# Decode of two layers over a key-value cache: the norm's factor applied to the projections' results, and a shorter wait ahead of them

## The chip, the cores and the metric

The kernel runs on one core of a Trainium2 chip. The metric is the device time of one execution in microseconds (us). The kernel before was run nine times; its time is the median of these.

## The reference

Eight rows (B = 8, one token each, D = 448) pass two times through an attention layer and an MLP layer with the same weights. All inputs are bfloat16. Cut to what matters:

```python
def ln(x): return (x - mean(x)) / sqrt(var(x) + 1e-5)

def A(x):                       # 16 query heads, 8 key/value heads of 256, 4096 positions
    q = (x @ wq)                # 448 -> 4096
    p = softmax(q . k_cache / 16)
    return (p . v_cache) @ wo   # 4096 -> 448

def Bmlp(x):
    h  = gelu(ln(x) @ w1); hs = shifted_along_the_sequence(h) @ w2
    x1 = x + hs                 # every shift leaves a sequence of length 1
    return x1 + gelu(ln(x1) @ w3) @ w4      # 448 -> 1792 -> 448

for layer in range(2):
    x = x + A(ln(x))
    x = x + Bmlp(ln(x))
```

The sequence has length one and each of the four groups is shifted by one or two places and filled with zeros, so hs is zero and x1 = x; w1 and w2 are not read. The MLP step is therefore x + ln(x) + gelu(ln(ln(x)) @ w3) @ w4. The norm of a norm is the same centred x with another factor.

## The kernel before

**The stream.** The work is a list of 128 pairs (layer, row, key/value head). A pair needs a key and a value cache of 2 MB each, loaded in halves of 1 MB into a ring of five buffers. All loads are issued by SyncE in one order; each waits until the buffer it overwrites has been used. Of each row, nine of the sixteen key halves stay in SBUF, transposed (`keep`), from layer 0 to layer 1, so that layer 1's pairs of heads 0 to 3 load only values, and head 4 half of its keys. The list alternates such light pairs with whole ones.

**A pair** (`attend`). In eight turns TensorE transposes four blocks of keys into PSUM (`tk`, L607), and VectorE (L614) and ScalarE (L612) copy them out by turns, to `ktr` or `keep`. Then come the scores (`ps`, L631), the maximum (VectorE L678, GpSimd L681), the exponential on ScalarE (L687), the sum on GpSimd (L692), and the product with the values (`pvb`, L705), copied to `ob` (L711), turned by TensorE (L723), summed to `os` (L726) and scaled to `oT` (L730). `output` multiplies one head's `oT` by wo (L457) and VectorE adds the result to x (L463); for the first five rows of layer 1 `outputs` does this for all heads at once (L473, L480).

**The jobs.** Everything that follows a row's last pair is a generator: `mix` (the MLP) and `queries` (the next layer's q). `pump`, called after every turn, every two scores and every product with values, advances the first job by one `yield`. At each `yield` the job's instructions issued so far stand on the engines' queues ahead of the pair's next ones, and every engine runs its queue in order. `Sched.op` adds the semaphores' waits. The first queries, of all eight rows, run through (`drain`) after the first pair's keys have been transposed; the last MLP, of rows 5 to 7, runs through at the end with nothing beside it. The MLP of rows 0 to 4 in layer 1 is one job among the last row's pairs.

**The norm before** (`layernorm`, `rsqrt`, `scaled`, `lift`). VectorE squares x (L346) and sums x and its square per partition (L347); GpSimd sums over the partitions (`partition_all_reduce`, L351). VectorE forms mean and variance (L355, L357, L359), for the MLP the second factor's argument (L365), the centred x (`xc`, L369), and the reciprocal root by a bit trick and three Newton steps (L327 to L338). Then L376 writes `lnT`, the centred x times the factor, for the MLP also `t1`, the first norm's result, and L491 adds that to x (`xres`). After WAIT empty steps `project` multiplies (L417). D = 448 is held as one block of 64 rows and three of 128; the 64-row block stands in the lower half of the partitions, and half of the weights' tiles have it in the upper half. `lift` moves lnT's 64 rows up by a matmul with the identity (L404) and a copy (L407). The queries are copied from PSUM to `qT` (L436 for one row, L445 for eight); the MLP's projection to `hb` (L501), on which the GELU works (L504 to L512). L521 is the second projection and L526 its sum with `xres`. At the very end x is transposed (L780), copied (L783) and stored (L785).

Of the kernel before, what the change touches and what calls it, by code (L numbers as in the profile page):

```python
# [3 lines left out]
P = 128  # L4
B = 8
D = 448
HQ = 16
# [6 lines left out]
KC = 4  # L14
NF = F // P
LN_EPS = 1e-5
# [9 lines left out]
N_REP = 24  # L26
N_MLP = 24
RATE = 1.0
WAIT = 5
N_PS = 2  # L30
N_SPARE = 2
N_ONCE = 5
# [99 lines left out]
def decode_two_layers(nc, A_x, A_k_cache, A_v_cache, A_wq, A_wo, B_w3, B_w4, out):  # L132
# [10 lines left out]
    def sb(name, shape, dt):  # L143
        return nc.alloc_sbuf_tensor(name, shape, dt), Res()
# [25 lines left out]
    lnT, r_ln = sb("lnT", [P, KC + 1, B], bf)  # L170
    r_lift = Res()
    sm, r_sm = sb("sm", [P, 8, 2 * B], f32)
    smi, r_smi = sb("smi", [P, 2 * B], i32)
    hb, r_hb = sb("hb", [P, NF, B], f32)
    hw, r_hw = sb("hw", [P, NF, B], f32)
# [20 lines left out]
    C_Y = 0  # L196
    C_H = 32
    C_Q = 160
    C_L = 480
    C_P = 448  # L200


# [120 lines left out]

    def rsqrt(src, dst, n):

        v, y, w, hv = sm[:, src, 0:n], sm[:, dst, 0:n], sm[:, 7, 0:n], sm[:, 6, 0:n]
        op("dve", lambda e: e.tensor_single_scalar(smi[:, 0:n], v.bitcast(i32), 1, ALU.arith_shift_right),  # L327
           reads=[r_sm], writes=[r_smi])
        op("dve", lambda e: e.tensor_scalar(smi[:, 0:n], smi[:, 0:n], -1, RSQRT_MAGIC, ALU.mult, ALU.add),
           reads=[r_smi], writes=[r_smi])  # L330
        op("dve", lambda e: e.tensor_single_scalar(hv, v, -0.5, ALU.mult), reads=[r_sm], writes=[r_sm])
        yield
        y0 = smi[:, 0:n].bitcast(f32)
        for i in range(3):
            a, r_a = (y0, r_smi) if i == 0 else (y, r_sm)
            op("dve", lambda e, a=a: e.tensor_tensor(w, a, a, ALU.mult), reads=[r_a], writes=[r_sm])
            op("dve", lambda e: e.tensor_tensor(w, w, hv, ALU.mult), reads=[r_sm], writes=[r_sm])  # L337
            op("dve", lambda e, a=a: e.scalar_tensor_tensor(y, w, 1.5, a, ALU.add, ALU.mult),  # L338
               reads=[r_sm, r_a], writes=[r_sm])
            yield  # L340

    def layernorm(lo, n, twice):

        x_ = xT[:, :, lo:lo + n]
        s = lambda k, a=0: sm[:, k, a * n:(a + 1) * n]
        op("dve", lambda e: e.tensor_tensor(xx[:, 1, :, lo:lo + n], x_, x_, ALU.mult), reads=[r_x], writes=[r_x])  # L346
        op("dve", lambda e: e.tensor_reduce(sm[:, 0, 0:2 * n].rearrange("p (k n) -> p k n", k=2),  # L347
                                            xx[:, :, :, lo:lo + n].rearrange("p k c n -> p k n c"),
                                            axis=AX.X, op=ALU.add),
           reads=[r_x], writes=[r_sm])  # L350
        op("pool", lambda e: e.partition_all_reduce(sm[:, 1, 0:2 * n], sm[:, 0, 0:2 * n], P, ReduceOp.add),  # L351
           reads=[r_sm], writes=[r_sm])
        yield
        yield
        one = lambda o, *a: op("dve", lambda e: e.tensor_single_scalar(o, *a), reads=[r_sm], writes=[r_sm])  # L355
        one(sm[:, 1, 0:2 * n], sm[:, 1, 0:2 * n], 1.0 / D, ALU.mult)
        op("dve", lambda e: e.scalar_tensor_tensor(s(2), s(1), -1.0, s(1), ALU.mult, ALU.mult),  # L357
           reads=[r_sm], writes=[r_sm])
        op("dve", lambda e: e.tensor_tensor(s(2), s(2), s(1, 1), ALU.add), reads=[r_sm], writes=[r_sm])  # L359
        one(s(4), s(2), 0.0, ALU.max)  # L360
        one(s(2), s(4), LN_EPS, ALU.add)
        yield
        if twice:

            op("dve", lambda e: e.scalar_tensor_tensor(s(2, 1), s(2), LN_EPS, s(4), ALU.mult, ALU.add),  # L365
               reads=[r_sm], writes=[r_sm])

        for hi, c0, c1 in ((P, 1, 4), (64, 0, 1)):
            op("dve", lambda e, hi=hi, c0=c0, c1=c1: e.tensor_tensor(  # L369
                xc[0:hi, c0:c1, 0:n], x_[0:hi, c0:c1, :],  # L370
                s(1)[0:hi].unsqueeze(1).to_broadcast([hi, c1 - c0, n]), ALU.subtract),
               reads=[r_x, r_sm], writes=[r_xc])
        yield from rsqrt(2, 3, 2 * n if twice else n)

    def scaled(dst, r_dst, a, n):
        op("dve", lambda e: e.tensor_tensor(dst[:, 0:KC, 0:n], xc[:, :, 0:n],  # L376
                                            bc(sm[:, 3, a * n:(a + 1) * n], n), ALU.mult),
           reads=[r_xc, r_sm], writes=[r_dst])

    def kr(kc):  # L380
        return P if kc > 0 else 64
# [17 lines left out]
            return w3[:, kc - 1, t * P:(t + 1) * P]  # L399
        return w3f[:, t % (NF // 2) * P:(t % (NF // 2) + 1) * P]  # L400

    def lift(n):

        op("pe", lambda e: e.matmul(mm[64:P, C_L:C_L + n], ident[0:64, 0:64], lnT[0:64, 0, 0:n],  # L404
                                    start=True, stop=True, skip_group_check=True),
           reads=[r_ident, r_ln], writes=[r_mm])
        op("dve", lambda e: e.tensor_copy(lnT[64:P, KC, 0:n], mm[64:P, C_L:C_L + n]),  # L407
           reads=[r_mm], writes=[r_lift])

    def project(cols, r_w, at, ts, upper, n):  # L410

        def f(e):
# [9 lines left out]
    def queries(lo, n):  # L422

        yield from layernorm(lo, n, False)
        scaled(lnT, r_ln, 0, n)
        for _ in range(WAIT):
            yield
        for h in range(HKV):
            for t in (4 * h, 4 * h + 2):
                project(wq_cols, wq_r, C_Q, range(t, t + 2), t >= 16, n)  # L430
                if t == 0:
                    lift(n)
                yield
            if n > 1:
                continue
            op("dve", lambda e, h=h: e.tensor_copy(  # L436
                qT[:, lo, :, 2 * h:2 * h + 2],
                mm[:, C_Q + 4 * h * B:C_Q + 4 * (h + 1) * B].rearrange("p (a c n) -> p n c a", n=B, c=2)[:, 0, :, :]),
               reads=[r_mm], writes=[r_q[lo][h]])
            ready[lo] = h + 1  # L440
            yield
            yield
        for c in range(2):
            if n > 1:
                op("dve", lambda e, c=c: e.tensor_copy(  # L445
                    qT[:, lo:lo + n, c, :],
                    mm[:, C_Q:C_Q + 32 * B].rearrange("p (a c n) -> p n c a", n=B, c=2)[:, 0:n, c, :]),
                   reads=[r_mm], writes=[r for b in range(lo, lo + n) for r in r_q[b]])

    def output(b, h):  # L450

# [31 lines left out]
    def mix(lo, n):  # L483

        y_ = mm[:, C_Y:C_Y + KC * B].rearrange("p (c n) -> p c n", n=B)[:, :, lo:lo + n]
        x_ = xT[:, :, lo:lo + n]
        yield from layernorm(lo, n, True)
        scaled(lnT, r_ln, 1, n)

        scaled(t1, r_t1, 0, n)  # L490
        op("dve", lambda e: e.tensor_tensor(xres[:, :, 0:n], x_, t1[:, :, 0:n], ALU.add),  # L491
           reads=[r_x, r_t1], writes=[r_xres])
        for _ in range(WAIT):
            yield
        for ts in (range(0, 2), range(2, 4), range(4, 7), range(7, 9), range(9, 11), range(11, 14)):
            project(w3_cols, w3_r, C_H, ts, ts[0] >= NF // 2, n)
            if ts[0] == 0:
                lift(n)
            yield
        h_, w_ = hb[:, :, 0:n], hw[:, :, 0:n]  # L500
        op("dve", lambda e: e.tensor_copy(  # L501
            h_, mm[:, C_H:C_H + NF * B].rearrange("p (t n) -> p t n", n=B)[:, :, 0:n]),
           reads=[r_mm], writes=[r_hb])
        op("dve", lambda e: e.scalar_tensor_tensor(w_, h_, GELU_C, h_, ALU.mult, ALU.mult),  # L504
           reads=[r_hb], writes=[r_hw])
        op("dve", lambda e: e.scalar_tensor_tensor(w_, w_, 1.0, h_, ALU.add, ALU.mult),
           reads=[r_hb, r_hw], writes=[r_hw])
        op("act", lambda e: e.activation(w_, w_, ACT.Tanh, scale=GELU_K), reads=[r_hw], writes=[r_hw])
        yield
        yield  # L510

        op("dve", lambda e: e.scalar_tensor_tensor(hT[:, :, 0:n], w_, 1.0, h_, ALU.add, ALU.mult),  # L512
           reads=[r_hb, r_hw], writes=[r_hT])
        yield
        yield
        for c in range(KC):
            def f(e, c=c):
                w = kr(c)
                last = None
                for t in range(NF):  # L520
                    last = e.matmul(room(w, C_Y + c * B + lo, n), w4[:, t, row0(c):row0(c) + w],  # L521
                                    copies(hT[:, t, 0:n], n), start=(t == 0), stop=(t == NF - 1), skip_group_check=True)
                return last
            op("pe", f, reads=[r_w4, r_hT], writes=[r_mm])
            yield
        op("dve", lambda e: e.scalar_tensor_tensor(x_, y_, 0.5, xres[:, :, 0:n], ALU.mult, ALU.add),  # L526
           reads=[r_mm, r_xres], writes=[r_x])
        yield
# [313 lines left out]
```

## Time and profile before

| | |
|---|---|
| median of nine runs | 1179.08 us (1178.33 to 1181.07) |
| the profiled execution | 1181.07 us, its span 1179.3 us |
| mean granted TensorE clock | 0.944 |
| TensorE busy (matmuls) | 947.2 us, 80% |
| VectorE busy | 490.7 us, 42%, 1819 instructions |
| ScalarE busy | 312.4 us, 26% |
| GpSimd busy | 105.4 us, 9% |
| transfers | 474.70 MB, mean 403 GB/s over the span |
| chain that ended last | DMA 47%, TensorE 36%, VectorE 10% |

The span runs from the first to the last instruction of the execution that the hardware profiler took. Busy times of engines overlap. In the profile PE is TensorE's matmuls, PEld its weight loads, DVE VectorE, ACT ScalarE, POOL GpSimd, SP SyncE; L417 is line 417 of the kernel before. In the changed kernel the same code has other line numbers.

### The profile page before, as it was taken

How to read it: one execution, taken by the hardware profiler on the slowest of the kernel's cores; microseconds unless marked ns; L12 is line 12 of the kernel's file. 1: busy time of each engine (PE TensorE's matmuls, PEld its weight loads, DVE VectorE, ACT ScalarE, POOL GpSimd, SP SyncE). 2: the span in 40 equal slices, each digit the busy share in tenths (PEclk: the TensorE clock that was granted, in tenths of full speed). 3: DMA queues.
4: the chain of work that ended last, by engine and by line, in shares of the span. 5: the costliest groups of instructions: out<-in, count | busy, mean ns of one | idle time of the engine just before them, and what ended most of it. 6: DMA issues, size and time to landing. Idle time of an engine off the chain costs nothing.

```text
span 1179.3 us, 42729 instructions
## 1 busy us (share of the span) xinstructions
PE 947.2 (80%) x19323; PEld 823.7 (70%) x19323; DVE 490.7 (42%) x1819; ACT 312.4 (26%) x891; POOL 105.4 (9%) x281
## 2 busy tenths in 40 slices
PE   2777888778877888778877887878877898888895
PEld 2766777667766776667766776767766777777784
DVE  2324543345333543354333533354334533454343
ACT  1223322223223222222222222232222222322220
POOL 0000001101001011001100011001110011001100
PEclk8879989899989999999999899999899998999896
DMA  9999999999999999999999999999999999999893
GB/s 351 384 416 420 419 387 420 419 420 419 417 417 416 412 420 405 419 420 411 417 416 420 384 395 413 419 420 413 413 419 420 404 409 419 419 418 395 350 402 144
DMA packets 70678, 474.70 MB, mean 403 GB/s; under 512 B 7248, under 2 KB 13280, under 8 KB 13792
## 3 DMA queue, kind: packets, MB, share of 16 engines
q1 hardware_dynamic: 70496, 471.97, 97.9%
q8 instruction: 151, 2.47, 0.8%
q14 instruction: 31, 0.25, 0.1%
HBM read 471.93 MB, written 0.01 MB: 400 GB/s over the span
## 4 chain that ended last, share of the span: by engine, by line
DMA 47%; PE 36%; DVE 10%; issue 5%; POOL 1%; ACT 0%; SPq 0%; POOLq 0%; ACTq 0%
DMA ring<-in_A_k_cache_dram 47%; PE tk L607 16%; PE ps L631 7%; PE pvb L705 5%; PE mm L457 3%; DVE ktr L614 3%; PE mm L417 2%; PE mm L521 1%; PE pvb L723 1%; DVE keep L614 1%; DVE oT L730 1%; DVE sm L355 1%; DVE os L726 1%; DVE sm L337 1%; DVE sm L338 1%
## 5 line engine op out<-in xcount | busy, mean ns | idle before, releaser
L607 PE MATMUL tk<-ident,ring 128*128 128x128 f32 x2944 | 412.5, 293 | 126.7 <-DMA ring<-in_A_k_cache_dram 125.2
L607 PEld LDWEIGHTS tk<-ident,ring 128*128 128x128 f32 x2944 | 347.2, 150 | 170.6 <-DMA ring<-in_A_k_cache_dram 161.6
L614 DVE COPY ktr<-tk 128x512 f32<-128x512 f32 x224 | 153.9, 690 | 187.9 <-PE tk L607 187.3
L612 ACT COPY ktr<-tk 128x512 f32<-128x512 f32 x224 | 129.9, 586 | 326.4 <-PE tk L607 326.3
L705 PE MATMUL pvb<-ring,pT 128*2 128x256 bf16 x4096 | 161.2, 277 | 31.0 <-DMA ring<-in_A_v_cache_dram 18.7
L631 PE MATMUL ps<-qT,keep 128*128 128x48 bf16 x4608 | 160.9, 184 | 5.7 <-issue 4.7
L631 PEld LDWEIGHTS ps<-qT,keep 128*128 128x128 bf16 x4608 | 145.7, 97 | 17.1 <-issue 11.2
L614 DVE COPY keep<-tk 128x512 f32<-128x512 f32 x144 | 99.6, 691 | 138.7 <-PE tk L607 138.0
L612 ACT COPY keep<-tk 128x512 f32<-128x512 f32 x144 | 84.4, 586 | 244.5 <-PE tk L607 244.5
L687 ACT ACTIVATE pT<-ps,nb 128x32 bf16<-128x32 f32 x256 | 76.6, 299 | 272.6 <-DVE nb L683 226.3
L631 PE MATMUL ps<-qT,ktr 128*128 128x48 bf16 x3584 | 129.9, 184 | 15.1 <-DVE ktr L614 6.7
L631 PEld LDWEIGHTS ps<-qT,ktr 128*128 128x128 bf16 x3584 | 115.5, 97 | 26.3 <-DVE ktr L614 18.5
L681 POOL PARTITION_ALL_REDUCE gm<-pm x128 | 45.6, 357 | 793.2 <-DVE pm L678 793.2
L705 PEld LDWEIGHTS pvb<-ring,pT 128*2 128x2 bf16 x4096 | 76.3, 82 | 55.5 <-DMA ring<-in_A_v_cache_dram 23.6
L457 PE MATMUL mm<-oT,wo_sb 128*128 128x24 bf16 (+1 forms) x1408 | 64.2, 187 | 11.9 <-DVE oT L730 6.0
L711 DVE COPY ob<-pvb 128x256 f32<-128x256 f32 x128 | 53.8, 420 | 42.0 <-PE pvb L705 41.3
L457 PEld LDWEIGHTS mm<-oT,wo_sb 128*128 128x128 bf16 (+1 forms) x1408 | 51.5, 101 | 24.6 <-DVE oT L730 20.7
L692 POOL PARTITION_ALL_REDUCE dn<-rs x128 | 51.3, 400 | 151.0 <-ACT pT L687 151.0
L723 PE MATMUL pvb<-ident,ob 128*128 128x128 f32 x256 | 53.7, 293 | 6.8 <-DVE ob L711 6.6
L678 DVE TENSOR_REDUCE pm<-ps 128x2 f32<-128x64 f32 x128 | 28.7, 224 | 70.0 <-PE ps L631 69.4
L417 PE MATMUL mm<-lnT,wq_sb 128*128 128x24 bf16 x864 | 48.5, 184 | 11.6 <-DVE lnT L376 9.1
L417 PEld LDWEIGHTS mm<-lnT,wq_sb 128*128 128x128 bf16 x864 | 40.3, 99 | 20.9 <-DVE lnT L376 9.4
(70 smaller groups left out, 491.0 us busy)
## 6 DMA issues: line engine op xcount, KB each, us to landing
ring<-in_A_v_cache_dram SPq DMA_DIRECT2D x256, 1024.0 KB, 10.3
ring<-in_A_k_cache_dram SPq DMA_DIRECT2D x184, 1024.0 KB, 10.5
wo_sb<-in_A_wo_dram SPq DMA_DIRECT2D x1, 3584.0 KB, 25.6
wq_sb<-in_A_wq_dram SPq DMA_DIRECT2D x3, 1024.0 KB, 11.5
w_sb<-in_B_w_dram SPq DMA_DIRECT2D x1, 1568.0 KB, 20.4
w_sb<-in_B_w_dram SPq DMA_DIRECT2D x3, 448.0 KB, 13.2
wqf_sb<-in_A_wq_dram SPq DMA_DIRECT2D x2, 256.0 KB, 14.9
w3f_sb<-in_B_w_dram SPq DMA_DIRECT2D x2, 112.0 KB, 14.3
```

The costliest lines, as they stand in the source:

```text
L417: last = e.matmul(room(P, at + t * B, n), cols(kc, t), copies(rhs, n), start=(kc == 1), stop=(kc == 0), skip_group_check=True)
L457: last = e.matmul(room(w, C_P + c, 1), wo[:, t, row0(c):row0(c) + w], copies(oT[:, t // 2, t % 2, b:b + 1], 1), start=(t == 4 * h), stop=( ...
L607: last = e.transpose(bank[:, j * P:(j + 1) * P], src[:, 4 * (f % 4) + j, :].bitcast(f32), ident4[:, :])
L612: op("act", lambda e: e.copy(flat, bank[:, :]), reads=[r_bank], writes=[r_kt])
L614: op("dve", lambda e: e.tensor_copy(flat, bank[:, :]), reads=[r_bank], writes=[r_kt])
L631: last = e.matmul(pst[:, at:at + 2 * N_REP].rearrange("p (r j) -> p r j", j=2), kt(i, c), repeated(qT[:, b, c, 2 * h:2 * h + 2]), start=(c ...
L681: op("pool", lambda e: e.partition_all_reduce(gm[q][0][:, :], pm[q][0][:, :], P, ReduceOp.max), reads=[pm[q][1]], writes=[gm[q][1]])
L687: return e.activation(pT[q][0][:, :, :].rearrange("p i j -> p j i")[:, j, :], pst[:, C_S:C_S + 2 * NI].rearrange("p (i j) -> p j i", j=2)[ ...
L692: op("pool", lambda e: e.partition_all_reduce(dn[q][0][:, :], rs[q][0][:, :], P, ReduceOp.add), reads=[rs[q][1]], writes=[dn[q][1]])
L705: last = e.matmul(pvb[at:at + 2, 0:DH], pT[q][0][:, a * HALF + i, :], v[:, i, :], start=(a == 0 and i < 4), stop=(a == 1 and i >= HALF - 4 ...
L711: op("dve", lambda e: e.tensor_copy(ob[:, :], pvb[:, 0:DH]), reads=[r_pv], writes=[r_ob])
L723: last = e.transpose(pvb[:, DH + c * P:DH + (c + 1) * P], ob[:, c * P:(c + 1) * P], ident4[:, :])
```

## The change

The order of the pairs, the ring, the loads and the split of the last MLP into five rows and three are the same in both kernels. What differs is the norm and what uses it.

- GpSimd's sum goes to a tile of its own, `sg`. `centered` forms x minus the mean from it and writes it straight into `lnT`, without the factor, ahead of the variance and the root. The projections run on that.
- The factor, one for each row, is multiplied into the projections' results: the copies to `qT` and `hb` become multiplications by it.
- `lift` goes. VectorE writes the upper 64 partitions of the lifted block itself, in two instructions of 32 partitions each.
- Five instructions of the variance become three, and the Newton step multiplies by -0.5 in passing, so that one instruction ahead of it goes.
- In `mix` the first norm's result and its sum with x are formed behind `hT`, from a second call of `centered`.
- WAIT, the empty steps ahead of the projections, goes from 5 to 3; `layernorm` with `rsqrt` has one more step than before.

```diff
-WAIT = 5
+WAIT = 3
...
+    sg, r_sg = sb("sg", [P, 2 * B], f32)
...
     def rsqrt(src, dst, n):
...
-        op("dve", lambda e: e.tensor_single_scalar(hv, v, -0.5, ALU.mult), reads=[r_sm], writes=[r_sm])
...
-            op("dve", lambda e: e.tensor_tensor(w, w, hv, ALU.mult), reads=[r_sm], writes=[r_sm])
+            op("dve", lambda e: e.scalar_tensor_tensor(w, w, -0.5, v, ALU.mult, ALU.mult), reads=[r_sm], writes=[r_sm])
...
     def layernorm(lo, n, twice):
...
-        op("pool", lambda e: e.partition_all_reduce(sm[:, 1, 0:2 * n], sm[:, 0, 0:2 * n], P, ReduceOp.add),
-           reads=[r_sm], writes=[r_sm])
-        yield
-        yield
-        (five instructions: mean, variance, clamp, eps)
-        yield
+        op("pool", lambda e: e.partition_all_reduce(sg[:, 0:2 * n], sm[:, 0, 0:2 * n], P, ReduceOp.add),
+           reads=[r_sm], writes=[r_sg])
+        yield
+        yield
+        centered(lnT, r_ln, lo, n)
+        yield
+        (three instructions: variance, clamp and eps)
+        for p in (0, 32):
+            op("dve", lambda e, p=p: e.scalar_tensor_tensor(
+                lnT[64 + p:96 + p, KC, 0:n], sg[p:p + 32, 0:n], -1.0 / D, x_[p:p + 32, 0, :], ALU.mult, ALU.add),
+               reads=[r_x, r_sg], writes=[r_lift])
         if twice:
+            op("dve", lambda e: e.tensor_single_scalar(s(4), s(4), 0.0, ALU.max), reads=[r_sm], writes=[r_sm])
             op("dve", lambda e: e.scalar_tensor_tensor(s(2, 1), s(2), LN_EPS, s(4), ALU.mult, ALU.add),
                reads=[r_sm], writes=[r_sm])
-        (two instructions that centre x into xc)
+        yield
         yield from rsqrt(2, 3, 2 * n if twice else n)
+
+    def centered(dst, r_dst, lo, n):
+        for hi, c0, c1 in ((P, 1, 4), (64, 0, 1)):
+            op("dve", lambda e, hi=hi, c0=c0, c1=c1: e.scalar_tensor_tensor(
+                dst[0:hi, c0:c1, 0:n], sg[0:hi, 0:n].unsqueeze(1).to_broadcast([hi, c1 - c0, n]), -1.0 / D,
+                xT[0:hi, c0:c1, lo:lo + n], ALU.mult, ALU.add),
+               reads=[r_x, r_sg], writes=[r_dst])
...
-    def scaled(dst, r_dst, a, n):
-    def lift(n):
...
     def queries(lo, n):
         yield from layernorm(lo, n, False)
-        scaled(lnT, r_ln, 0, n)
         for _ in range(WAIT):
             yield
...
-                if t == 0:
-                    lift(n)
...
-            op("dve", lambda e, h=h: e.tensor_copy(
+            op("dve", lambda e, h=h: e.tensor_tensor(
                 qT[:, lo, :, 2 * h:2 * h + 2],
                 mm[:, C_Q + 4 * h * B:...],
+                sm[:, 3, 0:1].unsqueeze(2).to_broadcast([P, 2, 2]), ALU.mult),
...
     def mix(lo, n):
         yield from layernorm(lo, n, True)
-        scaled(lnT, r_ln, 1, n)
-        scaled(t1, r_t1, 0, n)
-        op("dve", lambda e: e.tensor_tensor(xres[:, :, 0:n], x_, t1[:, :, 0:n], ALU.add),
-           reads=[r_x, r_t1], writes=[r_xres])
         for _ in range(WAIT):
             yield
...
-            if ts[0] == 0:
-                lift(n)
...
-        op("dve", lambda e: e.tensor_copy(h_, mm[:, C_H:...]), reads=[r_mm], writes=[r_hb])
+        op("dve", lambda e: e.tensor_tensor(h_, mm[:, C_H:...],
+            sm[:, 3, n:2 * n].unsqueeze(1).to_broadcast([P, NF, n]), ALU.mult),
+           reads=[r_mm, r_sm], writes=[r_hb])
...
         op("dve", lambda e: e.scalar_tensor_tensor(hT[:, :, 0:n], w_, 1.0, h_, ALU.add, ALU.mult),
            reads=[r_hb, r_hw], writes=[r_hT])
         yield
+        centered(xc, r_xc, lo, n)
+        op("dve", lambda e: e.tensor_tensor(t1[:, :, 0:n], xc[:, :, 0:n], bc(sm[:, 3, 0:n], n), ALU.mult),
+           reads=[r_xc, r_sm], writes=[r_t1])
+        op("dve", lambda e: e.tensor_tensor(xres[:, :, 0:n], x_, t1[:, :, 0:n], ALU.add),
+           reads=[r_x, r_t1], writes=[r_xres])
         yield
```

## The prediction

> **What bounds the kernel now.** I read the page's slices first, to see where the transfers run, then a table of windows for the stretches where they do not, then the chain of waits through the end, then the timelines of the start and of the one large hole, and last the list of waits.
>
> The page's slices of DMA share and of throughput:
>
> ```profile
> DMA  9999999999999999999999999999999999999893
> GB/s 351 384 416 420 419 387 420 419 420 419 417 417 416 412 420 405 419 420 411 417 416 420 384 395 413 419 420 413 413 419 420 404 409 419 419 418 395 350 402 144
> ```
>
> Each slice is 29.5 us. The DMA engines are full in all slices but two: the kernel is a stream of 472 MB that runs at about 420 GB/s when nothing holds it back, and what can be won is the stretch without transfers at the end, the hole in the 38th slice, and a few per cent where the rate drops.
>
> The table of windows (us, then busy time of PE, PEld, DVE, ACT and POOL, then granted clock, DMA share, GB/s):
>
> ```profile
> 30.00:45.00 15.00, 13.97 (x254) 12.80 (x252) 6.13 (x16) 4.85 (x14) 1.54 (x4) 0.80 1.06 393
> 150.00:195.00 45.00, 40.32 (x835) 35.92 (x832) 19.69 (x80) 11.79 (x34) 4.18 (x11) 0.89 1.00 399
> 1110.00:1120.00 10.00, 7.94 (x134) 6.83 (x135) 4.17 (x24) 1.71 (x6) 1.25 (x4) 0.66 0.62 212
> 1160.00:1179.30 19.30, 8.76 (x183) 6.24 (x171) 6.74 (x39) 0.24 (x1) 0.47 (x1) 0.50 0.02 7
> ```
>
> The last 19.3 us have no transfers: there a chain of dependent work on TensorE and VectorE alone sets the end, so what the change takes off that chain comes off the time whole. In the other stretches only what keeps the DMA engines from idling or slowing counts.
>
> The chain of waits through the last MLP (start, us, what):
>
> ```profile
> 1166.36 0.18 DVE sm L355
> ...
> 1170.12 0.19 DVE lnT L376
> 1170.31 0.05 issue
> 1170.35 0.39 PE mm L417 x8
> 1170.74 0.15 PE mm L404
> 1170.92 0.18 DVE lnT L407
> 1171.10 0.05 issue
> 1171.14 1.47 PE mm L417 x48
> 1172.63 0.21 DVE hb L501
> ...
> 1173.89 2.16 PE mm L521 x56
> ```
>
> One after the other: the norm's VectorE chain (1166.36 to 1170.30), the projection with the lift in it (1170.35 to 1172.6), the GELU, the second projection.
>
> **The change, part by part.** *The tail.* Before, GpSimd's sum is there at 1166.33 and hb starts at 1172.63: 6.27 us from L355's start. After, lnT is centred by the first two VectorE instructions, so TensorE projects while VectorE goes on to the root. The order of the changed build puts 20 VectorE instructions between the sum and hb: two that centre, three for the variance, two that lift, two for the second factor, two that seed the root, nine Newton steps. In the rows of before, an instruction that needs the one ahead of it starts 0.20 us later (L336 at 1168.32, L337 at 1168.52, L338 at 1168.72), one that does not 0.08 to 0.09 later (L331 at 1168.12 after L329 at 1168.04). Of the 20 steps to hb's start, 17 are dependent by the waits in the changed build and 3 are not: 17 x 0.20 + 3 x 0.09 = 3.67 us, so hb starts at about 1170.03. TensorE's side: lnT is whole at about 1166.8, the lifted columns after seven instructions at 1167.6; 56 matmuls at 1.47/48 = 0.031 us each are 1.7 us, done by about 1168.7, well ahead of VectorE. So the VectorE chain alone is late next, and the tail gains 1172.63 - 1170.03 = **2.6 us**. If I mis-paced the steps by 0.02 us each, it is 2.2.
>
> hb becomes a multiplication from PSUM in place of a copy. L501 took 0.20 us for 42 columns, and L480, which adds two tensors of which one is PSUM, 0.16 for 20: I take no difference, bounds -0.02 to +0.1.
>
> The four instructions that now follow hT (centre again, scale, add to the residual; 0.09 + 3 x 0.20 = 0.7 us) lie beside L521's 2.16 us of matmuls and cost nothing there; were the matmuls not above them, the tail would gain 1.9 instead. TensorE idles longer ahead of L521, about 2.5 us where it was 1.3. The granted clock is 0.50 in every window from 1161 to the end, so the wait finds nothing to slow down. The Trainium skill's "TensorE: Matmul & The Clock Gate" (Part 1) speaks against such a gap: the clock falls to half after an idle window of about 3.4 us. By that rule a kernel whose tail still ran at full clock could pay, as an estimate, half of the second projection, and most of this gain would be gone; the row of this case has the half already paid.
>
> *The start.* The same rearrangement stands ahead of the first scores. The timeline of SyncE:
>
> ```profile
> 17.66 0.44 SPq L312 DMA_DIRECT2D wo_sb<-in_A_wo_dram  x1
> 37.07 1.40 SPq L280 DMA_DIRECT2D ring<-in_A_v_cache_dram  x1
> ```
>
> SyncE issues nothing for 19 us, since its next load waits for the transposes of the second pair, which stand behind the queries on TensorE. Before: lnT at 26.36, 128 matmuls to 30.6, qT, first scores at 31.29. After: lnT at about 22.0, matmuls (3.39/120 = 0.028 us each, 3.6 us) to 25.7, and VectorE's chain of 18 instructions with two evictions of 0.68 ends near 26. The scores, and SyncE's next load, come some 4.5 us earlier. But the DMA engines do not idle in this stretch (share 1.06 from 30 to 45): wo and the chunks ahead of it keep them full. All that can be won is the drop from 420 to 393 GB/s, 15 x 27/420 = 0.96 us. The nearest row is the full DMA share, so I take 0.3, between 0 and 1.0. qT's two scalings of 128 columns stand at 0.29 us each as copies; I leave them. The Trainium skill's "VectorE: DVE Perf Modes" (the perf-mode tier table) says a copy from PSUM may run at up to twice the rate of a two-tensor operation; as an estimate that is 0.07 us for each of the two here and 0.02 for hb, against this change. No run here shows a multiplication of 128 columns from PSUM.
>
> *The stream between.* Per row the norm of the MLP keeps its 26 VectorE instructions (the residual's four move behind hT), that of the queries goes from 23 to 20: 27 fewer of 0.16 us over the kernel. 19 lifts (a matmul of 0.2 us and a copy each) go. Fewer steps and WAIT of 3 bring each row's queries one or two turns earlier; SyncE's order is the same in both builds, and so are the order of pairs and the split into five rows and three, which stand in both kernels. What VectorE's queue holds up shows in the waits (total us, times, longest):
>
> ```profile
> PE mm L457 <- DVE oT L730: 6.0, 5, 2.2
> PE ps L631 <- DVE sm L336: 3.6, 6, 0.7
> PE ps L631 <- DVE sm L365: 3.6, 7, 0.5
> ```
>
> 13 us over the whole kernel, most of it while the DMA share is full. The new order has two clumps of five or so instructions where there were two of five or six, and the first half of a residual's work later. I see no sign for either direction and take 0, with bounds of -3 and +3: a quarter of these 13 us each way.
>
> **The sum.** 2.6 + 0.3 + 0 = 2.9 us off. The profiled execution took 1181.07 us with a span of 1179.3, so 1.8 lies around the span; it was the slowest of nine, whose median is 1179.08. Taken from the median: **1176.2 us**. A measurement of this kernel can tell about 0.2% from no change, 2.36 us: faster means below 1176.7, slower above 1181.4.
>
> **The rivals.** *The hole closes or moves.* The timeline of TensorE shows what opens the hole of the 38th slice:
>
> ```profile
> 1108.98 0.47 PE L631 MATMUL ps<-qT,keep 128*128 128x48 bf16 x12
> 1112.06 0.98 PE L631 MATMUL ps<-qT,keep 128*128 128x48 bf16 x20 [2.60 <-issue]
> ```
>
> TensorE stops for 2.60 us in the middle of a group, for nothing that a semaphore explains; a 16 KB packet of the instruction queue starts at 1109.72. From 1110 to 1120 the rate is 212 GB/s, 5 us of transfer lost. The lifts' instructions are gone ahead of this point and jobs run a turn or two earlier, so the stop may fall where chunks are in hand. For: only this one of TensorE's stops of 0.7 to 2.6 us empties the DMA engines so far. Against: the rows' outputs and the norm of five rows still stand there, as dense. Gain up to 5, I price it at 3.7: 1172.5 us.
>
> *The gain is half eaten.* The tail lands, but the stream gives back 1 to 2 us, as TensorE's other stops shift: about 1177.7, no difference that can be told.
>
> *Slower: the residual's place.* In eight rows and the batch of five, the four instructions behind hT (0.7 us) now stand on VectorE's queue ahead of the next key eviction and of oT, on which the output matmuls wait. Where TensorE sets the pace, as from 150 to 195 (40.3 of 45 us busy, 399 GB/s), each may reach the stream whole: 9 x 0.7 = 6.3 us, 1182.5 us. It turns slower from (2.9 + 2.36)/9 = 0.58 us passed on by each. For: L457 waited up to 2.2 us for oT behind a norm. Against: before has the same work on the same queue, three instructions and the scaling, some turns earlier, and the DMA share there is 1.00.
>
> **How the numbers follow.** The forecast has 0.56 (1175.3 to 1177.2, of which a fifth is no difference), the closed hole 0.14, the half-eaten gain 0.20, the slower rival 0.10. Faster: 0.45 + 0.14 = 0.59; same: 0.11 + 0.20 = 0.31; slower 0.10. The range runs from the priced hole, 1172.5, to the forecast with the stream's +3 on it and with the low ends of tail and start (0.4 and 0.1 lost to pace and to hb, 0.3 not won), 1180.0; the slower rival and the rest of the hole are left out. The likeliest case's own range is 1175.3 to 1177.2.
>
> **What would show it.** In the last MLP: hb 3.6 to 3.8 us behind the first VectorE instruction after the sum, waiting for VectorE and not for TensorE; the residual's instructions inside L521's time. At the start: first scores near 27, SyncE's gap ending near 32.5, the first 45 us with hardly more bytes. Between: the same count of pairs, waits on oT near 6 us. I am wrong if hb waits for TensorE, if the last transfer lands more than 2 us earlier or later than before, or if TensorE stops in the tail for instructions.

## The result and the profile after

| | before | after |
|---|---|---|
| median, runs side by side | 1180.24 us (33 runs) | 1172.51 us (11 runs) |
| profiled execution, its span | 1181.07 us, 1179.3 us | 1173.25 us, 1171.5 us |
| mean granted TensorE clock | 0.944 | 0.943 |
| VectorE instructions | 1819 | 1792 |

The ratio is 0.9936, with a 95% interval of 0.9925 to 0.9947. Of some 1180 us that is 7.6 us less (6.3 to 8.9), where the forecast had 2.9. Faster was right. The size was not: 1172.51 us lies on the lower edge of the range, 1172.5 to 1180.0, and outside the likeliest case's own, 1175.3 to 1177.2.

The page's slices of the changed kernel:

```profile
DMA  9999999999999999999999999999999999999994
GB/s 350 385 415 419 419 407 417 421 418 417 407 420 420 416 412 406 419 420 404 418 415 419 414 418 399 420 419 413 414 418 415 411 417 419 414 419 402 384 399 169
```

The 8 in the 38th slice is gone, and 350 GB/s there has become 384. The table of windows (us, busy time of PE, PEld, DVE, ACT and POOL, granted clock, DMA share, GB/s):

```profile
30.00:45.00 15.00, 10.95 (x198) 9.88 (x195) 5.61 (x15) 4.72 (x14) 1.54 (x4) 0.96 1.06 392
150.00:195.00 45.00, 40.47 (x862) 34.89 (x861) 19.69 (x80) 11.80 (x35) 4.54 (x12) 0.92 1.01 410
1110.00:1120.00 10.00, 8.74 (x154) 7.84 (x143) 5.05 (x21) 2.52 (x7) 0.76 (x2) 0.83 1.00 395
1153.10:1171.50 18.40, 8.85 (x182) 6.36 (x182) 6.90 (x40) 0.24 (x1) 0.47 (x1) 0.52 0.05 20
```

The hole of 1110 to 1120 us, 212 GB/s at a DMA share of 0.62, is filled. The first 45 us move as much as before. In the table's last line the transfers have not quite ended: by the packets in the trace the last data land at 1155.7 us, and at 1161.1 in the kernel before, where the prediction let the stretch without transfers begin at 1160.

The chain of waits through the last MLP of the changed kernel:

```profile
1160.91 0.19 DVE lnT L378
...
1161.76 0.17 DVE lnT L364
...
1164.55 0.18 DVE sm L337
...
1164.82 0.21 DVE hb L488
...
1166.02 0.07 DVE xc L378
1166.09 2.15 PE mm L515 x56
1168.24 0.02 issue
1168.26 0.18 DVE xx L520
```

TensorE's projection (L412) is no longer in it: VectorE goes from the centred x (L378) through the root to hb (L488) without a break. That takes 3.91 us, where L355 to hb took 6.27.

**Where the 7.8 us between the two profiled executions lie.** I follow the bytes landed, added up from the packets in the trace. Each profile is one execution, and the differences are taken before rounding:

| stretch | before | after | difference |
|---|---|---|---|
| up to 449 MB | 1098.9 us | 1096.0 us | -2.9 |
| 449 to 465 MB, the last row | 44.6 us | 41.5 us | -3.1 |
| 465 MB to the last data | 17.6 us | 18.1 us | 0.6 |
| from there to the span's end | 18.2 us | 15.8 us | -2.4 |

The first 2.9 us are not shown to be the change's doing: two of the experiments' kernels issue the same instructions as before up to this point, and they arrive there at 1096.8 us (e1) and 1101.0 us (e8). The last 2.4 us are the tail. The 449 to 465 MB are the last row's pairs, among which stand the outputs and the MLP of rows 0 to 4. As will be seen, that stretch is short in every kernel that has the changed kernel's order there, and it holds the gain that I had not forecast.

### The profile page after: what moved, and what is told of

It is laid out like the page before. It is cut to its first block, busy times and chain, and to the rows that moved or that the text cites. A ratio compares the mean times of both kernels' runs of the same rounds, so it can differ in the third digit from the quotient of the medians.

```text
span 1171.5 us, 42672 instructions
## 1 busy us (share of the span) xinstructions
PE 950.7 (81%) x19304; PEld 830.2 (71%) x19304; DVE 488.1 (42%) x1792; ACT 312.3 (27%) x891; POOL 105.4 (9%) x281
## 4 chain that ended last, share of the span: by engine, by line
DMA 52%; PE 33%; DVE 9%; issue 4%; POOL 1%; ACT 1%; SPq 0%; POOLq 0%; DVEq 0%; ACTq 0%
DMA ring<-in_A_k_cache_dram 50%; PE tk L601 16%; PE ps L625 5%; PE pvb L699 4%; PE mm L451 3%; DVE ktr L608 3%; DMA ring<-in_A_v_cache_dram 2%; PE mm L515 1%; PE mm L412 1%; PE pvb L717 1%; DVE oT L724 1%; DVE os L720 1%; DVE keep L608 1%; POOL gm L675 1%; DVE sm L336 0%
## 5 line engine op out<-in xcount | busy, mean ns | idle before, releaser
L601 PE MATMUL tk<-ident,ring 128*128 128x128 f32 x2944 | 421.7, 297 | 128.0 <-DMA ring<-in_A_k_cache_dram 127.2
L601 PEld LDWEIGHTS tk<-ident,ring 128*128 128x128 f32 x2944 | 355.2, 152 | 172.4 <-DMA ring<-in_A_k_cache_dram 163.6
L699 PE MATMUL pvb<-ring,pT 128*2 128x256 bf16 x4096 | 157.6, 274 | 29.7 <-DMA ring<-in_A_v_cache_dram 21.4
L412 PE MATMUL mm<-lnT,wq_sb 128*128 128x24 bf16 x864 | 47.8, 184 | 5.1 <-DVE lnT L378 4.3
L412 PEld LDWEIGHTS mm<-lnT,wq_sb 128*128 128x128 bf16 x864 | 39.3, 98 | 14.9 <-issue 6.5
```

Source lines behind the costliest of these rows:

```text
L412: last = e.matmul(room(P, at + t * B, n), cols(kc, t), copies(rhs, n), start=(kc == 1), stop=(kc == 0), skip_group_check=True)
L601: last = e.transpose(bank[:, j * P:(j + 1) * P], src[:, 4 * (f % 4) + j, :].bitcast(f32), ident4[:, :])
L699: last = e.matmul(pvb[at:at + 2, 0:DH], pT[q][0][:, a * HALF + i, :], v[:, i, :], start=(a == 0 and i < 4), stop=(a == 1 and i >= HALF - 4 ...
```

## The experiments

All twelve kernels are built from one source with both forms of the norm in it. All switched off it issues the instructions of before, all on those of the changed kernel. Two functions choose. Most diffs below change their constants; those of e3 to e6, e11 and e12 are written as what they do to the kernel that they start from:

```python
def new(lo, n):     # does this job use the changed norm, the factor on the results, the later residual?
    if NEW_BATCH is not None and n == N_ONCE: return NEW_BATCH      # for e8
    return NEW_START if n == B else NEW_TAIL if (lo, n) == (N_ONCE, B - N_ONCE) else NEW_STREAM
def wait(lo, n):    # empty steps ahead of its projections
    if WAIT_LAST is not None and (lo, n) == (B - 1, 1): return WAIT_LAST
    return WAIT_NEW if new(lo, n) else WAIT_OLD
```

The steps matter because of the list of jobs. The last row's two jobs, its MLP of layer 0 and its queries for layer 1, stand ahead of the outputs and of the MLP of rows 0 to 4. A norm and its empty steps take 7 + 5 = 12 steps before and 8 + 3 = 11 after. So with two norms ahead of them, the outputs and the batch's norm come two steps earlier. Of each kernel I give its median and that of the runs of before beside it, then the ratio of the two kernels' runs with its 95% interval (not quite the quotient of the medians: e9's median is 1.4 us below before's at a ratio of 0.9997), and the time of the transfers from 449 to 465 MB in its profile; the table behind the last experiment shows what TensorE does in that stretch.

**e1: the tail alone.** The changed norm in the last MLP only.

```diff
-NEW_START, NEW_STREAM, NEW_TAIL = False, False, False
+NEW_START, NEW_STREAM, NEW_TAIL = False, False, True
```

> The new norm in the last MLP alone (rows 5 to 7 in layer 1); every other norm and the wait of 5 as before. Against the kernel before (1180.2 us). Both theories: the tail is worth its own chain, 2.3 us from the sum to the end in the changed kernel's profile, so 1177.9 us, ratio 0.998. If the tail were worth all of it: 1172.5.

1176.33 us beside 1179.21: 0.9975 (0.9963 to 0.9987), 2.9 us less; the last row takes 43.8 us. The tail is worth what the forecast gave it; it does not make up the 7.6 us.

**e2: the stream alone.** The changed norm with its three empty steps in every job but the first queries and the last MLP.

```diff
-NEW_START, NEW_STREAM, NEW_TAIL = False, False, False
+NEW_START, NEW_STREAM, NEW_TAIL = False, True, False
```

> The new norm, with its wait of 3, in the rows' MLPs and queries among the pairs, and in the batch of five; the first queries and the last MLP as before. Theory S (the stream gained, in its own jobs): 1180.2 - 5.3 = 1174.9 us, ratio 0.9955. Rival P (the two profiles differ in the stream by chance, and start and tail bring it all): 1179 to 1181.

1175.86 us beside 1179.21: 0.9971 (0.9960 to 0.9982), 3.4 us less; the last row takes 41.0 us. The term that I had put at 0 is as large as the tail. Tail and stream together make 6.3 of the 7.6 us, and the rest is inside the intervals.

**e3 and e4: is it the norm's shape or its steps?** The changed kernel with five empty steps (13 in all), and the kernel before with three (10 in all).

```diff
 # e3, from the changed kernel
-WAIT = 3
+WAIT = 5
 # e4, from the kernel before
-WAIT = 5
+WAIT = 3
```

> The changed kernel with its wait of 5 in place of 3. Theory N (the norm's new shape brings the stream's part, not the wait): unchanged, 1172.5 us, within 1. Theory W (the earlier jobs bring it): the stream's 5.3 us come back, 1177.8.

> The kernel before with its wait of 3 in place of 5, nothing else. Theory W: the stream's part comes from this alone, 1180.2 - 5.3 = 1174.9 us. Theory N: 1180.2, within 1; slower by 1 to 2 if TensorE then waits for the root, which the wait of 5 covered.

e3: 1177.24 us beside 1179.21, 0.9985 (0.9971 to 0.9998), last row 44.6 us: with two more steps the changed norm loses the stream's gain. e4: 1179.71 us, 1.0009 (0.9996 to 1.0021), last row 45.0 us: earlier is not simply better.

**e5 and e6: the steps exchanged.** The old norm with four empty steps (7 + 4 = 11, the changed kernel's count) and the changed norm with four (8 + 4 = 12, the count of before). In the stream TensorE's work then stands in the other kernel's order, the lifts aside.

```diff
 # e5, from the kernel before
-WAIT = 5
+WAIT = 4
 # e6, from the changed kernel
-WAIT = 3
+WAIT = 4
```

> The kernel before with a wait of 4 in place of 5, its norm unchanged. With the old norm's seven steps and four of waiting, every projection, and the batch's outputs in the last row, stands at the same place among the pairs' matmuls as in the changed kernel. Theory O (the order on TensorE brings the stream's part, above all that the batch's four dense groups of outputs alternate with transposes and no longer with scores): the stop of 2.6 us for instructions near 1110 is gone, 449 to 465 MB take about 41.5 us in place of 44.6, and the time is 1179.2 - 3.4 = 1175.8 us. Theory S (the new norm's shape brings it: fewer VectorE instructions, no lift): as before, 1179.2, within 1.

> The changed kernel with a wait of 4 in place of 3: TensorE's order is that of the kernel before, but for the lifts. Theory O: the stop of 2.6 us is back, and what is left is the tail and perhaps the start: 1179.2 - 2.9 = 1176.3 us, up to 1 less. Theory S: as the changed kernel, 1172.5 us, ratio 0.9936.

e5: 1176.72 us beside 1178.9, 0.9977 (0.9963 to 0.9990), last row 42.3 us. e6: 1176.26 us, 0.9973 (0.9960 to 0.9986), last row 43.9 us. The old norm has the stream's gain by one number in its source; the changed norm with the old count has the tail's gain and nothing more. That decides between shape and order: the order of the jobs carries the stream's part. It also settles the rival of the residual's place, since e6 has it in every row and shows no loss beside e1 (0.9973 and 0.9975).

**e7: the order, in the last row alone.** The kernel before; four empty steps only in the two jobs of row 7.

```diff
-WAIT_LAST = None
+WAIT_LAST = 4
```

> The kernel before with a wait of 4 in the last row's MLP and queries alone (row 7), so that only the batch's outputs and what follows move, to their place in the changed kernel. Theory O, the batch alone: 1175.8 us as with the wait of 4 everywhere. If the earlier rows share in it: between 1176 and 1179. Theory S: 1179.2.

1176.32 us beside 1178.9: 0.9974 (0.9962 to 0.9987), last row 40.7 us. Two steps in the last row bring about what the stream as a whole brings.

**e8 and e9: the changed norm elsewhere.** Only in the MLP of rows 0 to 4, and only in the first queries.

```diff
 # e8, from the kernel before
-NEW_BATCH = None
+NEW_BATCH = True
 # e9, from the kernel before
-NEW_START, NEW_STREAM, NEW_TAIL = False, False, False
+NEW_START, NEW_STREAM, NEW_TAIL = True, False, False
```

> The kernel before with the new norm in the batch's MLP alone (rows 0 to 4 in layer 1), its outputs where they were. Theory O: 1179.2 us, within 1, with the stop of 2.6 us. If it is the batch's norm on VectorE's queue, on which oT waits 2.2 us, that costs: 1179.2 - 2 = 1177.2 us.

> The new norm in the first queries of all eight rows alone; everything else as before. In the changed kernel's profile the first scores come 3.5 us or more earlier, but its transfers reach 15, 25 and 50 MB at the same times as before, within 0.1 us. Theory D (the transfers set the pace there): 1179.2 us, within 0.6, ratio 1.000. If the start is worth what tail and order leave over of the changed kernel's gain: 1179.2 - 1.3 = 1177.9 us.

e8: 1179.44 us beside 1178.9, 1.0007 (0.9990 to 1.0023), last row 45.6 us. e9: 1177.98 us beside 1179.37, 0.9997 (0.9979 to 1.0016), last row 43.6 us. No gain or loss can be told for either.

**e10: does the instruction stop make the hole?** The kernel before with 64 small matmuls more at the start, so that the 16 KB packets in which TensorE's instructions arrive end at other places in the last row.

```diff
-PAD = 0
+PAD = 64
```

> The kernel before with 64 small matmuls into an unused part of PSUM ahead of the first projections, where TensorE waits for the norm; they move every later TensorE instruction by half a 16 KB block of the instruction stream, and change no order. Theory I (the stop near 1110 is a block's fetch that no queued work covers, and its length makes the hole): the stop moves or changes length, and 449 to 465 MB take less time by what it loses, up to 2 to 3 us off: 1176 to 1177.5. Theory Q (the order sets it through oT's wait on VectorE's queue, 2.2 us, and the stop's place does not matter): 1179.2, within 1, and 44.6 us for these bytes.

The timeline of TensorE in e10:

```profile
1107.35 0.27 PE L742 MATMUL ps<-qT,ktr 128*128 128x48 bf16 x4 [1.37 <-issue]
...
1112.46 0.32 PE L742 MATMUL ps<-qT,keep 128*128 128x48 bf16 x6 [0.90 <-issue]
...
1119.46 0.72 PE L550 MATMUL mm<-oT,wo_sb 128*64 128x24 bf16 x16 [2.42 <-DVE oT L841]
```

Where before had one stop of 2.60 us, e10 has two of 1.37 and 0.90, and its stops for instructions come to 2.27 us in the last row, where before has 3.39. The time stays: 1178.96 us beside 1179.37, 0.9996 (0.9986 to 1.0005), last row 44.2 us. In e5 a stop of 2.15 us remains and the gain is there. So the one long stop, which the prediction's rival had made the cause, does not decide by itself. The wait on oT is still in e10's third line.

**e11: the outputs in smaller pieces.** From the changed kernel, each of the four groups of 32 output matmuls in two halves, with a step between.

```diff
-        for c in range(KC):
+        for c, half in [(c, half) for c in range(KC) for half in (0, 1)]:
...
-                for t in range(32):
+                for t in range(16 * half, 16 * half + 16):
```

> The changed kernel with the batch's four groups of 32 output matmuls cut into eight of 16, one at each step, so that the dense matmuls alternate more finely with the pairs' own. Theory I: the stops of 1.05 and 0.85 us shrink, 1 to 2 us less than the changed kernel: 1170.5 to 1171.5, ratio 0.992. Theory Q: the norm comes four steps later and meets other evictions; 1171.5 to 1174.5, no gain that can be told.

1176.29 us beside 1179.37: 0.9970 (0.9959 to 0.9980), last row 44.3 us. It keeps the tail's gain and loses the stream's: the four steps more push the batch's norm back.

**e12: the outputs' place or the norm's place.** In e7 both the outputs and the MLP of rows 0 to 4 stand two steps earlier. Here the outputs stay there, and the MLP, its norm first, goes back.

```diff
-WAIT_LAST = None
+WAIT_LAST = 4
...
     def mix(lo, n):
+        for _ in range(BATCH_DELAY if n == N_ONCE else 0):      # BATCH_DELAY = 2
+            yield
```

> The kernel before with four empty steps in place of five in the last row's jobs, as in e7, and two more empty steps ahead of the norm of rows 0 to 4 alone. The four groups of outputs then stand where the changed kernel has them, one after each of four transposing turns, and the norm and the projections of rows 0 to 4 stand beside the same turns as in the kernel before. Theory 'outputs': the place of the four groups of outputs is what wins. Then the transfers from 449 to 465 MB take 40.5 to 42.5 us as in e5 and e7, the time is about 2.7 us below before's (ratio 0.997 to 0.998), though oT waits 2 us behind the norm. Theory 'norm': the norm's place, two turns earlier, is what wins, since oT no longer waits behind it. Then the stretch takes 44 to 45 us, oT waits 2.0 to 2.4 us, and the ratio is 0.9995 to 1.0005.

1178.34 us beside 1179.14: 0.9997 (0.9981 to 1.0013), last row 45.9 us. No gain can be told any more, and what was taken back is the place of the MLP of rows 0 to 4, not the outputs'. The norm is the first part of that MLP; its projections went back with it and were not tried alone. This is the weakest of the readings. The intervals of e7 and e12 overlap between 0.9981 and 0.9987. Four of e12's twelve executions took 1182.9 to 1183.8 us and the other eight 1176.2 to 1178.9; the profiled one, at 1182.92, is one of the four, so that its 45.9 us are more than the kernel usually takes, and the eight may have kept part of the gain. The wait on oT, 2.42 us against 0.98 in e7, goes with the order: it is 2.13 to 2.42 us in the profiles of all nine kernels that have this norm as late as before or later.

What the norm's place does to oT is seen on VectorE. The timeline of VectorE in the kernel before, the end of the batch's norm:

```profile
1120.37 0.69 DVE L614 COPY ktr<-tk 128x512 f32<-128x512 f32 x1
1120.97 0.16 DVE L336 TENSOR_TENSOR sm<-sm 128x10 f32<-128x10 f32 x1
1121.17 0.17 DVE L337 TENSOR_TENSOR sm<-sm 128x10 f32<-128x10 f32 x1
1121.37 0.17 DVE L338 SCALAR_TENSOR_TENSOR sm<-sm 128x10 f32<-128x10 f32 x1
1121.57 0.18 DVE L376 TENSOR_TENSOR lnT<-xc,sm 128x20 bf16<-128x20 f32 x1
1121.67 0.17 DVE L376 TENSOR_TENSOR t<-xc,sm 128x20 f32<-128x20 f32 x1
1121.88 0.18 DVE L491 TENSOR_TENSOR xres<-xx,t 128x20 f32<-128x20 f32 x1
1121.98 0.17 DVE L726 TENSOR_REDUCE os<-pvb 128x4 f32<-128x16 f32 x1
1122.18 0.18 DVE L730 TENSOR_TENSOR oT<-os,rc 128x4 bf16<-128x4 f32 x1
```

and in the changed kernel:

```profile
1113.13 0.17 DVE L336 SCALAR_TENSOR_TENSOR sm<-sm 128x10 f32<-128x10 f32 x1
1113.34 0.17 DVE L337 SCALAR_TENSOR_TENSOR sm<-sm 128x10 f32<-128x10 f32 x1
1113.42 0.69 DVE L608 COPY ktr<-tk 128x512 f32<-128x512 f32 x1
1114.02 0.17 DVE L720 TENSOR_REDUCE os<-pvb 128x4 f32<-128x16 f32 x1
1114.22 0.18 DVE L724 TENSOR_TENSOR oT<-os,rc 128x4 bf16<-128x4 f32 x1
```

Before, the norm from the mean on (1116.40 us) stood between one pair's oT (1113.78) and the next one's, which waited behind it and behind two evictions of keys. In the changed kernel its first half, from the centring at 1106.66 us to 1108.24, is done ahead of the previous pair's oT (1108.36), and only the root from 1110.53 on stands between the two, with two evictions as before. The wait itself, in the timelines of TensorE, one line each of before, the changed kernel, e7 and e12:

```profile
1122.41 0.72 PE L457 MATMUL mm<-oT,wo_sb 128*64 128x24 bf16 x16 [2.19 <-DVE oT L730]
```

```profile
1114.45 0.72 PE L451 MATMUL mm<-oT,wo_sb 128*64 128x24 bf16 x16 [1.26 <-DVE oT L724]
```

```profile
1115.84 0.72 PE L549 MATMUL mm<-oT,wo_sb 128*64 128x24 bf16 x16 [0.98 <-DVE oT L840]
```

```profile
1122.33 0.72 PE L551 MATMUL mm<-oT,wo_sb 128*64 128x24 bf16 x16 [2.42 <-DVE oT L844]
```

The table of windows for 449 to 465 MB, of before, the changed kernel, e7 and e12 in this order:

```profile
1098.90:1143.60 44.70, 38.68 (x878) 34.14 (x876) 18.77 (x76) 10.42 (x30) 3.51 (x9) 0.92 0.92 362
```

```profile
1096.00:1137.50 41.50, 37.25 (x862) 33.03 (x860) 18.19 (x73) 10.34 (x29) 3.52 (x9) 0.96 1.00 388
```

```profile
1096.60:1137.40 40.80, 36.40 (x864) 32.12 (x861) 18.44 (x74) 10.19 (x30) 3.47 (x9) 1.00 0.99 396
```

```profile
1099.10:1144.90 45.80, 40.42 (x875) 35.87 (x874) 19.08 (x77) 10.41 (x30) 3.47 (x9) 0.89 0.95 352
```

In this stretch TensorE is the bound: its timelines name no wait for data in it, but for 0.20 us in e5. Its busy time and its stops add up to nearly all of the stretch: 38.7 + 5.8 of 44.6 us before, 37.2 + 3.9 of 41.5 after, 36.4 + 4.2 of 40.7 in e7, 40.4 + 5.0 of 45.9 in e12. So the changed kernel gains here by 1.9 us less standing still and 1.4 us less busy time. The longest wait on oT is 0.9 us shorter, and the stops marked `issue`, which no semaphore explains (the stops for instructions), come to 1.90 us where they came to 3.39; some small waits grew.

The busy time goes with the granted clock, which in these stretches is 1.00 or 0.50 and nothing between. The table of windows of before, and then of the changed kernel, at the half clock:

```profile
1111.20:1118.00 6.80, 5.94 (x105) 4.84 (x106) 2.22 (x13) 0.76 (x4) 0.76 (x2) 0.50 0.46 165
```

```profile
1116.10:1119.50 3.40, 3.40 (x42) 3.21 (x39) 0.75 (x2) 0.59 (x1) 0.00 (x0) 0.50 1.01 422
```

Before, the half clock begins inside the stop of 2.60 us (1109.46 to 1112.06) and lasts until 1118.0; most of the hole of 1110 to 1120 us, 165 GB/s, is this stretch. The same for all kernels, from the clock in their traces:

| kernel | 449 to 465 MB, us | longest wait on oT | all stops | busy | mean clock | at half clock, us |
|---|---|---|---|---|---|---|
| e7 | 40.7 | 0.98 | 4.2 | 36.4 | 1.00 | 0 |
| e2 | 41.0 | 1.25 | 3.4 | 37.3 | 1.00 | 0 |
| after | 41.5 | 1.26 | 3.9 | 37.2 | 0.96 | 3.4 |
| e5 | 42.3 | 1.01 | 4.1 | 37.8 | 0.96 | 3.4 |
| e9 | 43.6 | 2.20 | 6.0 | 37.3 | 0.96 | 3.4 |
| e1 | 43.8 | 2.13 | 5.9 | 37.5 | 0.96 | 3.4 |
| e6 | 43.9 | 2.32 | 5.9 | 37.6 | 0.96 | 3.4 |
| e10 | 44.2 | 2.42 | 5.5 | 38.4 | 0.96 | 3.4 |
| e11 | 44.3 | 2.15 | 5.7 | 38.3 | 0.92 | 6.8 |
| before | 44.6 | 2.19 | 5.8 | 38.7 | 0.92 | 6.8 |
| e3 | 44.6 | 2.16 | 6.6 | 37.7 | 0.92 | 6.8 |
| e4 | 45.0 | 1.58 | 4.3 | 40.0 | 0.92 | 6.8 |
| e8 | 45.6 | 2.31 | 6.4 | 38.9 | 0.93 | 6.8 |
| e12 | 45.9 | 2.42 | 5.0 | 40.4 | 0.89 | 10.2 |

Each line is one execution; those of e8 and e12 took 4.7 and 4.6 us over their kernel's median, all others between 1.2 below and 2.1 above, before included (2.0 above the median of its first nine runs). Every kernel with a wait of over 2 us on oT takes 43.6 us or more, and every one below 43 us has none over 1.3; e4 has 1.58 us, another 1.64 on `ob`, and 45.0 us. But the wait is only part of it: e2 waits on oT twice, 0.94 and 1.25 us, as long in sum as before, and is among the shortest. The half clock puts the fourteen in the same order as their times: 40.7 and 41.0 us without it, 41.5 to 44.2 with 3.4 us of it, 44.3 to 45.6 with 6.8, 45.9 with 10.2. Among the six with 3.4 us the time goes with the stops: 3.9 and 4.1 us of them in the changed kernel and e5, 5.5 to 6.0 in e9, e1, e6 and e10, which take 1.3 to 2.7 us more. So the order of the jobs is shown to carry the gain; that it does so through the wait on oT alone is not. What sets where the clock is halved, and whether another execution of the same kernel would show it there, was not tested. No kernel of these was faster than the changed one.

## Why the prediction was right and wrong

**The tail: right.** Forecast 2.6 us, measured 2.9 us alone (e1, 1.5 to 4.4) and 6.27 - 3.91 = 2.36 us in the chain of the profile. hb waits for VectorE, as said. Of the pace, the 0.24 us missing are in two places: the step into the first lift (L364, from 1161.57 to 1161.76) and the one out of the second (from 1161.95 to 1162.13), both without a wait in the build, took 0.19 and 0.18 us where I had counted 0.09 each, and hb starts 0.27 us after the last Newton step and not 0.20. hb as a multiplication costs nothing: 213 ns for 42 columns, and the row of before has 223 for the copy. The prediction's remark that at a full clock most of the gain would be gone is too strong by its own terms: half of the second projection's 2.16 us is 1.1, less than half of 2.6.

```profile
L488 DVE TENSOR_TENSOR hb<-mm,sm x10: 172/173/213, 141.5 to 1164.8; 128x14 f32<-128x14 f32 x8, 128x70 f32<-128x70 f32 x1, 128x42 f32<-128x42 f32 x1
```

**The residual behind hT: right.** In the last MLP it runs under L515, and TensorE waits longer ahead of that, 3.00 us where I said 2.5. The changed kernel's timelines of VectorE and then of TensorE:

```profile
1166.30 0.17 DVE L505 TENSOR_TENSOR t<-xc,sm 128x12 f32<-128x12 f32 x1
1166.51 0.17 DVE L507 TENSOR_TENSOR xres<-xx,t 128x12 f32<-128x12 f32 x1
1168.26 0.17 DVE L520 SCALAR_TENSOR_TENSOR xx<-mm,xres 128x12 f32<-128x12 f32 x1 [1.59 <-PE mm L515]
```

```profile
1166.08 2.15 PE L515 MATMUL mm<-hT,w_sb 128*64 128x24 bf16 x56 [3.00 <-DVE xc L378]
```

L520 waits for TensorE and not for xres, which has been there for 1.6 us. The line names xc as what L515 waited for, but L515 starts 0.28 us after hT's instruction does, as L521 did before. In the rows of the stream, the slower rival needed more than 0.58 us from each residual; e2 and e6 show no loss.

**The start: right in its place, worth nothing that can be told.** The first scores start at 27.41 us (forecast: near 27), and SyncE's gap ends at 32.29 us (forecast 32.5). The timelines of TensorE and SyncE:

```profile
27.41 1.78 PE L625 MATMUL ps<-qT,keep 128*128 128x48 bf16 x40 [1.37 <-DVE qT L438]
```

```profile
32.29 5.55 SPq L280 DMA_DIRECT2D ring<-in_A_v_cache_dram  x1
```

The issue that came 4.8 us earlier then took 5.55 us where it had taken 1.40, ahead of engines that were full: the transfers reach 50 MB at 127.6 us, and at 127.5 before. e9 measures 0.9997. I had 0.3 us for it. The scalings to qT took 292 ns, the copies 291. The Trainium skill's "VectorE: DVE Perf Modes" (the perf-mode tier table) gives copies from PSUM a cap of twice the rate of a two-tensor operation. The prediction's estimate went by that cap, but the same page, under the table ("Why PSUM operands drop a tier"), allows fp32 from PSUM no more than the single rate, and qT and hb are both read from PSUM as fp32: 292 ns as multiplications and 291 as copies, 213 and 223, so the page and the measurement agree.

**The stream between: the step that failed.** "I see no sign for either direction and take 0, with bounds of -3 and +3." It measured -3.4 us alone (e2, -2.1 to -4.7), at the bound, and that is where the forecast's 2.9 us fell short. The term was put at nothing on a count of instructions; what moved the time was the order of the jobs in the last row (e5, e7). A sign of it was in view. The prediction's own list of waits had the one of 2.2 us on oT, "behind a norm", and its own part on the change says that queries come "one or two turns earlier". I used the wait against the change (in the slower rival), and did not look where the changed order puts that norm against that pair's oT: the wait there went from 2.19 to 1.26 us. The list of waits of the changed kernel:

```profile
PE mm L451 <- DVE oT L724: 4.8, 6, 1.8
```

The total I named as the thing to watch fell only from 6.0 to 4.8 us. It could not tell the gain: of the 3.1 us in the last row the wait on oT is 0.9, and the rest is fewer stops for instructions and less time at the half clock, neither of which the prediction had in this term.

**The rival of the hole.** It named the right stretch, and its 1172.5 us is the measured time to 0.01 us. That is luck: it counted from 1179.08 us, and the runs of before beside the changed kernel have 1180.24, so that it had 6.6 us where 7.6 were measured; and the range reached down to 1172.5 only because this rival, at a chance of 0.14, was its lower end. As for its cause, one long stop for instructions, that is not shown: breaking the stop up (e10) changes nothing, and keeping one of 2.15 us (e5) does no harm to the gain. By what I had said would make me wrong, the last data landing more than 2 us earlier than before, the forecast's case did fail: they land 5.4 us earlier, and 3.1 us are won in the last row.

## What to carry to other kernels

An edit of a helper that many jobs share changes its count of steps, and with that the place of everything that queues behind it: look in the order of the changed build at where the largest waits of the profile now stand, before taking the stretch as unchanged. A wait behind another job's small VectorE instructions can count in the time where the engine that waits is the bound, as TensorE is in the last row here; ask of each wait in which stretch it lies, and of each stretch how much of it runs at a lower clock. Where a norm's factor is one number for each row, it can be applied to the projection's result: the matmuls then run beside the root and leave the chain, and the multiplication cost here what the copy did.

## What the runs showed of the hardware

**Stops for instructions.** TensorE stopped for up to 2.62 us at places where a semaphore explains nothing, in dense groups of small matmuls in the last row. In e6, from its timeline of TensorE:

```profile
1109.23 0.33 PE L741 MATMUL ps<-qT,keep 128*128 128x48 bf16 x7 [2.62 <-issue]
```

The instruction queue moves 16 KB packets there every 4 to 9 us, of 0.9 to 1.3 us each, beside the data queues. The Trainium skill's "Runtime: NRT & Kernel Launch" (Instruction fetch mechanics) says that instructions come in blocks of 16 KiB and that the crossing is mostly hidden; in the last row of before these stops make 3.4 of 44.6 us. That a late block is the cause was not shown.

**Half clock without a long stop.** In the last row TensorE's granted clock fell to 0.50 for 3.4, 6.8 or 10.2 us in twelve of fourteen profiles, though no stop there is longer than 2.62 us. In e7, with stops of up to 1.05 us, and in e2, with up to 1.25, it stayed at 1.00; in the changed kernel, with up to 1.26, it fell.

**Executions drift.** Before, e1 and e8, with the same instructions up to 449 MB, reach that point at 1098.9, 1096.8 and 1101.0 us. A difference of 3 us in a stretch of two single profiles, as the -2.9 us up to 449 MB here, is not evidence; it took the medians of eleven or more runs of each kernel and the same stretch in fourteen profiles to tell the last row from the rest.
